# A gated feed-forward kernel on one core: TensorE in program order, and a new order of the first stage

## The chip, the cores and the metric

The kernel runs on one core of one Trainium2 chip. The metric is the device time of one execution in microseconds. Before the change it is 559.42 us, the median of three runs (558.79 to 560.9).

The engines are called PE or TensorE (matmuls; PEld is its weight load), DVE or VectorE, ACT or ScalarE, POOL or GpSimd, and SP or SyncE, which here only issues transfers.

## The reference

x is 2048 x 1024, w_gate and w_up are 1024 x 3584, w_down is 3584 x 1024, all in bf16.

```python
g = jnp.einsum("bsd,df->bsf", x, w_gate)
u = jnp.einsum("bsd,df->bsf", x, w_up)
h = _gelu(g) * u
return jnp.einsum("bsf,fd->bsd", h, w_down)
```

## The kernel before

The kernel replaces eight block products by seven (a Strassen-Winograd scheme), at the price of sums of blocks, which other engines make. It goes over x in two passes of 1024 rows, each of two chunks of 512. A **unit** makes two blocks of 128 columns of h for both chunks, for gate and up: 7 groups of 8 matmuls. `t` are sums of blocks of x (made once a pass on VectorE), `s` are sums of blocks of weights (made for each unit, on GpSimd from the second unit on). Then a **down** stage multiplies h by w_down in the same manner.

The tile framework builds the program. For engines listed in `ORDER` the instructions stay in program order; the builder orders the others itself, before the program runs. TensorE and ScalarE are not in the list:

```python
ORDER = {ENG.SP, ENG.DVE, ENG.Pool}
...
ctx.enter_context(tc.manual_schedule(engines=ORDER))
...
kpool = ctx.enter_context(tc.tile_pool(name="k", bufs=SLOTS))   # 52 slots for sums and copies
wpool = ctx.enter_context(tc.tile_pool(name="w", bufs=3))       # three units' weights
bank = [psum.tile([P, N], f32, name=f"bank{i}") for i in range(8)]
even, odd, cc, dd = bank[0:2], bank[2:4], bank[4:6], bank[6:8]
```

The sums. `dve` and `pool` are tensor_tensor on VectorE and GpSimd (recorded as L90 and L93), `cast` and `snap` are ScalarE copies (L102 and L107), all matmuls outside the transposes are L111.

```python
def make_t(xT):
    t1, t2, t3, t4, tb = [], [], [], [], []
    for k in range(KH):                       # KH = 4
        b11, b12, b22 = xT[0][:, k], xT[1][:, k], xT[1][:, KH + k]
        t1.append(new(dve, b12, b11, SUB, "t1"))
        t2.append(new(dve, b22, t1[k], SUB, "t2"))
    for k in range(KH):
        t3.append(new(dve, xT[1][:, KH + k], xT[1][:, k], SUB, "t3"))
        tb.append(cast(xT[1][:, KH + k], "tb"))
    for k in range(KH):
        t4.append(new(dve, xT[0][:, KH + k], t2[k], SUB, "t4"))
    return t1, t2, t3, t4, tb
# make_s(w, eng): s1, s2, s3, s4 (two of each, on eng) and sa (two casts), in the same way
```

One unit. `e`, `c` and `d` are pairs of PSUM banks; `add(c, p1)` makes two VectorE sums.

```python
def unit(u, banks, xT, w, s, t, after_p5, aside):
    ...
    e, c, d = banks
    for i in GU: product(e[i], w[:, i, :KH, :P], b11, True)      # plain
    p1 = [snap(e[i], "p1") for i in GU]
    for i in GU: product(c[i], w[:, i, KH:, :P], b21, True)      # plain
    g, up = add(c, p1)
    for i in GU: product(e[i], s2[i], t2, False)
    times(2 * u, 0, gelu(g), up)                                 # hT <- g * up, VectorE
    aside(0)
    u2 = [snap(e[i], "u2") for i in GU]
    c = d
    for i in GU: product(c[i], s1[i], t1, True)                  # P5
    p5 = [snap(c[i], "p5") for i in GU]
    after_p5()            # next unit's s on GpSimd, the load of the weights after it
    for i in GU: product(e[i], s3[i], t3, False)
    g, up = new(dve, e[0], p5[0], ADD, "sum", dtype=f32), banks[1][1]
    dve(up, e[1], p5[1], ADD)
    for i in GU: product(c[i], s4[i], tb, False)
    times(2 * u + 1, 1, gelu(g), up)
    aside(1)
    g, up = add(c, u2)
    for i in GU: product(e[i], sa[i], t4, False)
    times(2 * u, 1, gelu(g), up)
    aside(2)
    times(2 * u + 1, 0, gelu(e[0]), e[1])
```

`aside` makes sums of w_down blocks on VectorE (`m`, three for each of 14 blocks, in the first pass), which go through a DRAM tile `td` to the down stage. `making(u)` says which of them a unit makes: one or two.

The start. Unit 0 is done without the scheme ("plain"), so that TensorE has work while the first sums are made:

```python
xn0 = load_x(0)                  # 4 transfers of 256 KB
# wf: unit 0's weights, 8 transfers of 128 KB
xn1 = load_x(1)
w = load_w(1)                    # 2 transfers of 512 KB
for _ in range(NWARM):           # 8
    nc.tensor.matmul(bank[3], lhsT=warm[:, :P], rhs=warm, start=True, stop=True)
turn(xT, xn0, 0)                 # 32 transposes to banks 4-7, copies on VectorE and ScalarE
JI = [(j, i) for j in range(2) for i in range(2)]
ps = bank[0:4]
for k in range(0, NKB, 2):
    for p, (j, i) in zip(ps, JI):
        plain(p, i, j, 0, [k, k + 1])
s = make_s(w, dve)
turn(xT, xn1, 1)
for j in range(2):
    times(j, 0, gelu(ps[2 * j]), ps[2 * j + 1])
t = make_t(xT)
ps = bank[0:2] + bank[6:8]
for p, (j, i) in zip(ps, JI):
    plain(p, i, j, 1, range(NKB))
for j in range(2):
    times(j, 1, gelu(ps[2 * j]), ps[2 * j + 1])
...
fetch_wd(0)
ahead = load_w(2)
# then the units 1 to 13 and the down stage, and the second pass
```

Of the kernel before, what the change touches and what calls it, by code (L numbers as in the profile page):

```python
# [10 lines left out]
def kernel(  # L11
# [22 lines left out]

    nc = tc.nc
    ENG = mybir.EngineType
    ORDER = {ENG.SP, ENG.DVE, ENG.Pool}
    P = nc.NUM_PARTITIONS
    bf16 = mybir.dt.bfloat16
    f32 = mybir.dt.float32  # L40
# [10 lines left out]
    NKB = Dm // P  # L51
    KH = NKB // 2
# [31 lines left out]


    bank = [psum.tile([P, N], f32, name=f"bank{i}") for i in range(8)]
    even, odd, cc, dd = bank[0:2], bank[2:4], bank[4:6], bank[6:8]

    def dve(out, a, b, op):
        nc.vector.tensor_tensor(out=out, in0=a, in1=b, op=op)  # L90
# [4 lines left out]
    def new(eng, a, b, op, name, shape=None, dtype=None):  # L95
        t = slot(shape or [P, N], dtype or f32r, name)
        eng(t, a, b, op)
        return t

    def cast(src, name, shape=None):  # L100
        t = slot(shape or [P, N], f32r, name)
        nc.scalar.copy(out=t, in_=src)  # L102
        return t
# [10 lines left out]

    def load_w(u):
        f0 = u * 2 * P
        w = wpool.tile([P, 2, NKB, 2 * P], bf16, name="w")
        for i, src in enumerate((w_gate, w_up)):  # L120
            nc.sync.dma_start(
                out=w[:, i],
                in_=src[:, f0 : f0 + 2 * P].rearrange("(ko ki) f -> ki ko f", ki=P),
            )
        return w

    def make_t(xT):
        t1, t2, t3, t4, tb = [], [], [], [], []
        for k in range(KH):
            b11, b12, b22 = xT[0][:, k], xT[1][:, k], xT[1][:, KH + k]  # L130
            t1.append(new(dve, b12, b11, SUB, "t1"))
            t2.append(new(dve, b22, t1[k], SUB, "t2"))
        for k in range(KH):
            t3.append(new(dve, xT[1][:, KH + k], xT[1][:, k], SUB, "t3"))
            tb.append(cast(xT[1][:, KH + k], "tb"))
        for k in range(KH):
            t4.append(new(dve, xT[0][:, KH + k], t2[k], SUB, "t4"))
        return t1, t2, t3, t4, tb

    def make_s(w, eng):  # L140
        s1, s2, s3, s4, sa = [], [], [], [], []
        sh = [P, KH, P]
        for i in range(2):
            a21, a22 = w[:, i, :KH, P:], w[:, i, KH:, P:]
            s1.append(new(eng, a21, a22, ADD, "s1", sh))
        for i in range(2):
            s2.append(new(eng, s1[i], w[:, i, :KH, :P], SUB, "s2", sh))
        for i in range(2):
            s3.append(new(eng, w[:, i, :KH, :P], w[:, i, :KH, P:], SUB, "s3", sh))
            sa.append(cast(w[:, i, KH:, P:], "sa", sh))  # L150
        for i in range(2):
            s4.append(new(eng, w[:, i, KH:, :P], s2[i], SUB, "s4", sh))
        return s1, s2, s3, s4, sa

    def gelu(src):
        g = slot([P, N], f32, "g")
# [4 lines left out]
        dve(hT[:, fb // NJ, fb % NJ, c, :], g, u, MUL)  # L161

    def unit(u, banks, xT, w, s, t, after_p5, aside):
        s1, s2, s3, s4, sa = s
        t1, t2, t3, t4, tb = t
        GU = range(2)

        def product(ps, lhs, rhs, start):
            for k in range(KH):
                matmul(ps, lhs[:, k, :], rhs[k], start and k == 0, k == KH - 1)  # L170

        def add(ps, other):

            g = new(dve, ps[0], other[0], ADD, "sum", dtype=f32)
            dve(ps[1], ps[1], other[1], ADD)
            return g, ps[1]

        b11 = [xT[0][:, k, :] for k in range(KH)]
        b21 = [xT[0][:, KH + k, :] for k in range(KH)]
        e, c, d = banks  # L180
        for i in GU:
            product(e[i], w[:, i, :KH, :P], b11, True)
        p1 = [snap(e[i], "p1") for i in GU]
        for i in GU:
            product(c[i], w[:, i, KH:, :P], b21, True)
        g, up = add(c, p1)
        for i in GU:
            product(e[i], s2[i], t2, False)
        times(2 * u, 0, gelu(g), up)
        aside(0)  # L190
        u2 = [snap(e[i], "u2") for i in GU]
        c = d
        for i in GU:
            product(c[i], s1[i], t1, True)
        p5 = [snap(c[i], "p5") for i in GU]
        after_p5()
        for i in GU:
            product(e[i], s3[i], t3, False)
        g, up = new(dve, e[0], p5[0], ADD, "sum", dtype=f32), banks[1][1]
        dve(up, e[1], p5[1], ADD)  # L200
        for i in GU:
            product(c[i], s4[i], tb, False)
        times(2 * u + 1, 1, gelu(g), up)
        aside(1)
        g, up = add(c, u2)
        for i in GU:
            product(e[i], sa[i], t4, False)
        times(2 * u, 1, gelu(g), up)
        aside(2)
        times(2 * u + 1, 0, gelu(e[0]), e[1])  # L210
# [84 lines left out]
    for j in range(NJ):  # L295
        at(AT12[j], load12, j)
        at(AT12S[j], make12, j)
        at(AT73[j] - 3, fetch73, j)
        at(AT73[j], make73, j)
        at(52 + 0.7 * j, load4, j)  # L300
        at(56 + 0.5 * j, make_sa, j)
    moves = [(c, ko) for ko in range(NKB) for c in range(2)]
    sa = {}

# [111 lines left out]
            )  # L416
    xn1 = load_x(1)
    w = load_w(1)
    for _ in range(NWARM):
        nc.tensor.matmul(bank[3], lhsT=warm[:, :P], rhs=warm, start=True, stop=True)  # L420
    turn(xT, xn0, 0)

    def plain(ps, i, j, c, kos):
        for ko in kos:
            matmul(
                ps,
                wf[:, i, ko, j * P : (j + 1) * P],
                xT[c][:, ko, :],
                ko == 0,
                ko == NKB - 1,  # L430
            )

    JI = [(j, i) for j in range(2) for i in range(2)]
    ps = bank[0:4]
    for k in range(0, NKB, 2):
        for p, (j, i) in zip(ps, JI):
            plain(p, i, j, 0, [k, k + 1])
    s = make_s(w, dve)
    turn(xT, xn1, 1)
    for j in range(2):  # L440
        times(j, 0, gelu(ps[2 * j]), ps[2 * j + 1])
    t = make_t(xT)
    ps = bank[0:2] + bank[6:8]
    for p, (j, i) in zip(ps, JI):
        plain(p, i, j, 1, range(NKB))
    for j in range(2):
        times(j, 1, gelu(ps[2 * j]), ps[2 * j + 1])

    def making(u):

        return {1: [0], 2: [1, 2], 3: [3], 4: [4, 5]}.get(u, [u + 1] if 4 < u < NU - 1 else [])

    nxt = {}
    fetch_wd(0)
    ahead = load_w(2)
    for ip in range(NPASS):
        for u in range(1 if ip == 0 else 0, NU):
            js = making(u) if ip == 0 else []

            def prepare():  # L460
                nonlocal ahead
                nxt["w"], nxt["s"] = ahead, None
                if u + 1 < NU:
                    nxt["s"] = make_s(ahead, pool)
                if u + 2 < NU:
                    ahead = load_w(u + 2)
                for j in making(u + 1) if ip == 0 else []:
                    fetch_wd(j)

            def aside(part):  # L470
                if len(js) == 1:
                    keep(js[0], part)
                elif js and part != 1:
                    for n in range(3):
                        keep(js[part // 2], n)
                    if part == 0:
                        store_made(js[0])

            if ip == 0 and making(u - 1):
                store_made(making(u - 1)[-1])  # L480
            unit(u, (odd if u % 2 else even, cc, dd), xT, w, s, t, prepare, aside)
            if u + 1 < NU:
                w, s = nxt["w"], nxt["s"]

        last = ip == NPASS - 1
        got, nxt = {}, {}

        def more(step):

            nonlocal ahead  # L490
            if last:
                return
            if step == 0:
                xT[:] = new_x()
            if step >= 0 and step % 2 == 0 and step // 2 < len(moves):
                c, ko = moves[step // 2]
                r0 = (2 * (ip + 1) + c) * N
                nc.sync.dma_start_transpose(
                    out=xT[c][:, ko, :], in_=x2[r0 : r0 + N, ko * P : (ko + 1) * P]
                )  # L500
            if step == 50:
                got["w"], ahead = load_w(0), load_w(1)
            if step == 58:
                got["s"] = make_s(got["w"], dve)
            if step == 62:
                got["t"] = make_t(xT)

        down(ip, even + cc, dd + odd, last, more)
        even, odd, cc, dd = odd, even, dd, cc
        if not last:  # L510
            w, t, s = got["w"], got["t"], got["s"]
# [29 lines left out]
```

## Time and profile before

| | value |
|---|---|
| median time | 559.42 us |
| span of the profiled execution | 558.6 us |
| TensorE busy | 541.4 us (97%) |
| VectorE busy | 367.7 us (66%) |
| ScalarE busy | 247.5 us (44%) |
| GpSimd busy | 242.6 us (43%) |
| moved by transfers | 93.30 MB, mean 167 GB/s |

The page of a profile lists the busy time of each engine, then the span in 40 equal slices (a digit is the busy share in tenths), and groups of instructions by line, engine and tile. Further views give the waits of an engine by releaser ("waited for: us in total, times, longest us"), the instructions in order of time (start, duration, what it is), and the busy time in chosen stretches.

### The profile page before, as it was taken

What the parts mean: (1) busy time and instruction counts of PE and PEld (TensorE: products, weight loads), DVE (VectorE), ACT (ScalarE), POOL (GpSimd) and SP (SyncE); (2) the same over time, 40 slices, a digit from 0 to 9 for tenths busy, and PEclk for the clock granted to TensorE, in tenths of its full rate; (3) what the DMA queues carried; (4) which work ended last, traced back from release to release, by engine and by line L of the source; (5) the groups of instructions that cost most, each with busy time, mean ns of one, the idle gap of its engine ahead of it and who ended that gap; (6) DMA issues with size and microseconds to landing.
All of it is one profiled execution on the core that took longest, in us unless ns stands there. A gap on an engine that the chain in (4) does not pass through costs nothing.

```text
span 558.6 us, 7422 instructions
## 1 busy us (share of the span) xinstructions
PE 541.4 (97%) x2398; PEld 381.1 (68%) x2432; DVE 367.7 (66%) x533; ACT 247.5 (44%) x430; POOL 242.6 (43%) x206
## 2 busy tenths in 40 slices
PE   5969999999999999999999999999999999999997
PEld 3436766767667764788877777777667775478885
DVE  1797978788777778388695545555545548757730
ACT  2514545455555521044535555555555551114531
POOL 0433596998788100000048766677777700000000
PEclk9998999999999999999999999999999999999999
DMA  8533667776666299977935333222222049554562
GB/s 254 160 85 122 215 219 235 216 226 172 169 171 208 100 306 301 281 231 213 297 118 152 88 108 103 79 76 76 76 76 75 2 143 377 176 196 123 162 203 90
DMA packets 104391, 93.30 MB, mean 167 GB/s; under 512 B 12960, under 2 KB 88736, under 8 KB 104352
## 3 DMA queue, kind: packets, MB, share of 16 engines
q1 hardware_dynamic: 104352, 92.82, 55.8%
q8 instruction: 20, 0.33, 0.3%
q14 instruction: 19, 0.16, 0.1%
HBM read 75.50 MB, written 15.20 MB: 162 GB/s over the span
## 4 chain that ended last, share of the span: by engine, by line
PE 89%; DMA 4%; DVE 4%; issue 1%; ACT 1%; SPq 0%; DVEq 0%; ACTq 0%
PE bank L111 88%; DMA td<-m 2%; DVE m L90 2%; DMA xn<-in_x_dram 2%; DVE hT L90 1%; DVE t L90 1%; ACT g L157 0%; DVE sum L90 0%; PE bank L399 0%; SPq L391 0%; DVE xT L402 0%; ACT sa L102 0%; ACT st L362 0%; ACT u L107 0%; SPq L411 0%
## 5 line engine op out<-in xcount | busy, mean ns | idle before, releaser
L93 POOL TENSOR_TENSOR s<-w 128x512 fp32r<-128x512 bf16 x100 | 122.7, 1246 | 203.5 <-DVE t L90 103.0
L111 PE MATMUL bank<-t,s 128*128 128x512 f32 x648 | 162.1, 405 | 4.9 <-DVE hT L90 4.4
L111 PEld LDWEIGHTS bank<-t,s 128*128 128x128 f32 x648 | 123.1, 191 | 35.0 <-DVE hT L90 4.8
L111 PE MATMUL bank<-xT,w 128*128 128x512 bf16 x468 | 111.6, 380 | 2.1 <-DVE xT L402 0.2
L157 ACT ACTIVATE g<-sum 128x512 f32<-128x512 f32 x81 | 51.2, 632 | 108.8 <-DVE sum L90 106.5
L107 ACT COPY p<-bank 128x512 f32<-128x512 f32 x124 | 70.4, 590 | 53.4 <-PE bank L111 52.3
L90 DVE TENSOR_TENSOR hT<-g,bank 128x512 bf16<-128x512 f32 x112 | 76.7, 687 | 18.6 <-PE bank L111 8.5
L111 PEld LDWEIGHTS <-w 128*128 128x128 bf16 x496 | 44.2, 98 | 60.5 <-issue 14.5
L90 DVE TENSOR_TENSOR sum<-bank,p 128x512 f32<-128x512 f32 x54 | 37.2, 688 | 72.4 <-PE bank L111 72.3
L93 POOL TENSOR_TENSOR s<-w,s 128x512 fp32r<-128x512 bf16 x50 | 61.8, 1260 | 0.0
L93 POOL TENSOR_TENSOR s<-s,w 128x512 fp32r<-128x512 f32 x50 | 60.9, 1240 | 0.4 <-PE bank L111 0.3
L111 PE MATMUL bank<-q 128*128 128x512 f32 x240 | 59.1, 389 | 0.0
L111 PE MATMUL bank<-t,sa 128*128 128x512 f32 x216 | 58.6, 413 | 0.0
L111 PE MATMUL bank<-tb,s 128*128 128x512 f32 x216 | 53.4, 389 | 0.0
L111 PEld LDWEIGHTS bank<-q 128*128 128x128 f32 x240 | 45.1, 188 | 9.3
L111 PE MATMUL bank<-raw,hT 128*128 128x512 bf16 x218 | 48.7, 379 | 0.3
L111 PEld LDWEIGHTS bank<-t,sa 128*128 128x128 f32 x216 | 40.7, 188 | 10.5
L111 PEld LDWEIGHTS bank<-tb,s 128*128 128x128 f32 x216 | 40.7, 188 | 8.6
L107 ACT COPY u<-bank 128x512 f32<-128x512 f32 x62 | 35.3, 588 | 22.6 <-PE bank L111 22.2
L90 DVE TENSOR_TENSOR q<-hT 128x512 fp32r<-128x512 bf16 x56 | 38.4, 687 | 10.3 <-PE bank L111 9.1
L102 ACT CAST tb<-raw 128x512 fp32r<-128x512 bf16 x28 | 17.0, 625 | 61.2 <-PE bank L111 31.4
L90 DVE TENSOR_TENSOR bank<-bank,p 128x512 f32<-128x512 f32 x54 | 37.6, 696 | 8.3 <-PE bank L111 6.9
(42 smaller groups left out, 455.0 us busy)
## 6 DMA issues: line engine op xcount, KB each, us to landing
raw<-in_w_down_dram SPq DMA_DIRECT2D x84, 256.0 KB, 4.8
q<-td SPq DMA_DIRECT2D x60, 256.0 KB, 5.1
w<-in_w_gate_dram SPq DMA_DIRECT2D x27, 512.0 KB, 5.9
w<-in_w_up_dram SPq DMA_DIRECT2D x27, 512.0 KB, 7.2
td<-m SPq DMA_DIRECT2D x14, 768.0 KB, 4.5
w<-td SPq DMA_DIRECT2D x6, 1024.0 KB, 8.1
out_dram<-st SPq DMA_DIRECT2D x32, 128.0 KB, 2.5
xn<-in_x_dram SPq DMA_DIRECT2D x8, 256.0 KB, 4.7
```

Of the source, the lines that this page charges most:

```text
L90: nc.vector.tensor_tensor(out=out, in0=a, in1=b, op=op)
L93: nc.gpsimd.tensor_tensor(out=out, in0=a, in1=b, op=op)
L102: nc.scalar.copy(out=t, in_=src)
L107: nc.scalar.copy(out=t, in_=ps)
L111: nc.tensor.matmul(ps, lhsT=lhs, rhs=rhs, start=start, stop=stop, skip_group_check=True)
L157: nc.scalar.activation(g, src, ACT.Gelu_apprx_tanh)
```

## The change

It keeps every product and every sum and changes their order. TensorE joins the engines that keep program order. In the first stage the transposes of the second chunk of x are put in the middle of the first plain chunk, between its two halves. The first s and t sums are made name by name in the order in which unit 1 uses them, with the evacuations of the plain banks between them, and s4 and t4 only inside unit 1. ScalarE keeps program order in this stage. The banks are assigned so that unit 1 takes the banks of the first plain chunk. The load of unit 2's weights is moved from the start into unit 1, and is issued by ScalarE after the p1 copies; with it moves the start of GpSimd's sums, which need these weights. The w_down sums are spread anew: one a unit from unit 2 on, two in units 6, 8 and 10. Two lists of steps in the down stage are shifted.

```diff
-    ORDER = {ENG.SP, ENG.DVE, ENG.Pool}
+    ORDER = {ENG.SP, ENG.DVE, ENG.Pool, ENG.PE}
-    even, odd, cc, dd = bank[0:2], bank[2:4], bank[4:6], bank[6:8]
+    even, odd, cc, dd = bank[6:8], bank[0:2], bank[2:4], bank[4:6]
...
-    def load_w(u):
+    def load_w(u, queue=nc.sync):
...
+            if queue is not nc.sync:
+                tc.keep_in_program_order(got)
...    (make_s and make_t: the same sums, made by name: s.make("s1", "s2"); t1 all four, then t2 all four, ...)
         p1 = [snap(e[i], "p1") for i in GU]
+        aside(-1)
...
-        at(52 + 0.7 * j, load4, j)
-        at(56 + 0.5 * j, make_sa, j)
+        at(49 + 0.65 * j, load4, j)
+        at(54 + 0.55 * j, make_sa, j)
...
+    s, t = sums_s(w, dve), sums_t(xT)
+    with tc.manual_schedule(engines={ENG.Activation}):
+        for _ in range(NWARM):
+            nc.tensor.matmul(bank[3], lhsT=warm[:, :P], rhs=warm, start=True, stop=True)
+        turn(xT, xn0, 0)
+        plain(bank[0:4], 0, range(0, KH))
+        turn(xT, xn1, 1)
+        plain(bank[0:4], 0, range(KH, NKB))
+        s.make("s1", "s2")
+        t.make("t1", "t2")
+        finish(bank[0:4], 0)          # two gelu, two hT
+        t.make("t3", "tb")
+        s.make("s3", "sa")
+        plain(bank[4:8], 1, range(NKB))
+        finish(bank[4:8], 1)
...
-        return {1: [0], 2: [1, 2], 3: [3], 4: [4, 5]}.get(u, [u + 1] if 4 < u < NU - 1 else [])
+        steps = [[], []]
+        for n in range(2, NU - 1):
+            first = sum(map(len, steps))
+            steps.append([first, first + 1] if n in (6, 8, 10) else [first])
+        return steps[u] if u < NU - 1 else []
...
-    fetch_wd(0)
-    ahead = load_w(2)
+    ahead = None
...
             def aside(part):
+                nonlocal ahead
+                if ahead is None:
+                    ahead = load_w(2, nc.scalar)
+                if part == 0 and "s4" not in s:
+                    s.make("s4")
+                    t.make("t4")
+                if part < 0:
+                    return
```

More of the change, by code (lines that the diff above doesn't have):

```diff
@@ L120, in load_w @@
         for i, src in enumerate((w_gate, w_up)):
-            nc.sync.dma_start(
+            got = queue.dma_start(
                 out=w[:, i],
@@ L124, in load_w @@
             )
-        return w
-    def make_t(xT):
[L128 to L138, printed above, removed]
@@ L140, in make_s @@
-    def make_s(w, eng):
[L141 to L153, printed above, removed]
+            if queue is not nc.sync:
+                tc.keep_in_program_order(got)
@@ new lines, in load_w, with make, sums_t @@
+        return w
+    class Sums(dict):
+        def make(self, *names):
+            for name in names:
+                self[name] = self["how"][name](self)
+    def sums_t(xT):
+        K = range(KH)
+        lo, hi = [[xT[c][:, k] for k in K] for c in range(2)], [
+            [xT[c][:, KH + k] for k in K] for c in range(2)
+        ]
+        return Sums(
+            how={
+                "t1": lambda q: [new(dve, lo[1][k], lo[0][k], SUB, "t1") for k in K],
+                "t2": lambda q: [new(dve, hi[1][k], q["t1"][k], SUB, "t2") for k in K],
+                "t3": lambda q: [new(dve, hi[1][k], lo[1][k], SUB, "t3") for k in K],
+                "t4": lambda q: [new(dve, hi[0][k], q["t2"][k], SUB, "t4") for k in K],
+                "tb": lambda q: [cast(hi[1][k], "tb") for k in K],
+            }
+        )
@@ new lines, in sums_s @@
+    def sums_s(w, eng):
+        GU = range(2)
+        sh = [P, KH, P]
+        a11, a21 = [[w[:, i, :KH, h : h + P] for i in GU] for h in (0, P)]
+        a12, a22 = [[w[:, i, KH:, h : h + P] for i in GU] for h in (0, P)]
+        return Sums(
+            how={
+                "s1": lambda q: [new(eng, a21[i], a22[i], ADD, "s1", sh) for i in GU],
+                "s2": lambda q: [new(eng, q["s1"][i], a11[i], SUB, "s2", sh) for i in GU],
+                "s3": lambda q: [new(eng, a11[i], a21[i], SUB, "s3", sh) for i in GU],
+                "s4": lambda q: [new(eng, a12[i], q["s2"][i], SUB, "s4", sh) for i in GU],
+                "sa": lambda q: [cast(a22[i], "sa", sh) for i in GU],
+            }
+        )
@@ L155, in gelu @@
+    def make_t(xT):
+        t = sums_t(xT)
+        t.make("t1", "t2", "t3", "tb", "t4")
+        return t
+    def make_s(w, eng):
+        s = sums_s(w, eng)
+        s.make("s1", "s2", "s3", "sa", "s4")
+        return s
     def gelu(src):
@@ L163, in unit @@
     def unit(u, banks, xT, w, s, t, after_p5, aside):
-        s1, s2, s3, s4, sa = s
-        t1, t2, t3, t4, tb = t
         GU = range(2)
@@ L187, in unit @@
         for i in GU:
-            product(e[i], s2[i], t2, False)
+            product(e[i], s["s2"][i], t["t2"], False)
         times(2 * u, 0, gelu(g), up)
@@ L193, in unit @@
         for i in GU:
-            product(c[i], s1[i], t1, True)
+            product(c[i], s["s1"][i], t["t1"], True)
         p5 = [snap(c[i], "p5") for i in GU]
@@ L197, in unit @@
         for i in GU:
-            product(e[i], s3[i], t3, False)
+            product(e[i], s["s3"][i], t["t3"], False)
         g, up = new(dve, e[0], p5[0], ADD, "sum", dtype=f32), banks[1][1]
@@ L201, in unit @@
         for i in GU:
-            product(c[i], s4[i], tb, False)
+            product(c[i], s["s4"][i], t["tb"], False)
         times(2 * u + 1, 1, gelu(g), up)
@@ L206, in unit @@
         for i in GU:
-            product(e[i], sa[i], t4, False)
+            product(e[i], s["sa"][i], t["t4"], False)
         times(2 * u, 1, gelu(g), up)
@@ L418 @@
     w = load_w(1)
[L419 to L447, printed above, removed]
-    def making(u):
-        return {1: [0], 2: [1, 2], 3: [3], 4: [4, 5]}.get(u, [u + 1] if 4 < u < NU - 1 else [])
+    def plain(ps, c, kos):
+        for k in range(kos.start, kos.stop, 2):
+            for p, (j, i) in zip(ps, [(j, i) for j in range(2) for i in range(2)]):
+                for ko in (k, k + 1):
+                    matmul(
+                        p,
+                        wf[:, i, ko, j * P : (j + 1) * P],
+                        xT[c][:, ko, :],
+                        ko == 0,
+                        ko == NKB - 1,
+                    )
@@ new lines, in finish @@
+    def finish(ps, c):
+        for j in range(2):
+            times(j, c, gelu(ps[2 * j]), ps[2 * j + 1])
+    s, t = sums_s(w, dve), sums_t(xT)
[13 more added lines that the diff above has]
+        finish(bank[4:8], 1)
```

## The prediction

> **What bounds the kernel now.** First the page's busy totals and its forty slices.
>
> ```profile
> PE 541.4 (97%) x2398; PEld 381.1 (68%) x2432; DVE 367.7 (66%) x533; ACT 247.5 (44%) x430; POOL 242.6 (43%) x206
> ...
> PE   5969999999999999999999999999999999999997
> PEclk9998999999999999999999999999999999999999
> ```
>
> TensorE is the bound, and it is full everywhere except in the first three slices (14 us each) and the last. Busy is not yet useful, though: a busy TensorE at half clock looks the same, so I read the waits of TensorE next, and then the first 50 us in stretches (columns: PE, PEld, DVE, ACT, POOL busy, granted clock, DMA share, GB/s).
>
> ```profile
> PE bank L399 <- DMA xn<-in_x_dram: 5.1, 2, 4.8
> PE bank L111 <- DVE hT L90: 4.4, 1, 4.4
> PE bank L420 <- DVE warm L382: 1.2, 1, 1.2
> ```
>
> ```profile
> 7.20:11.96 4.76, 0.00 (x0) 0.00 (x1) 0.02 (x1) 1.01 (x1) 0.00 (x0) 1.00 0.91 282
> ...
> 36.60:41.00 4.40, 0.01 (x1) 0.01 (x1) 4.40 (x9) 0.00 (x0) 0.00 (x0) 0.82 0.00 0
> ```
>
> ```profile
> 12.00:15.40 3.40, 3.06 (x25) 2.52 (x27) 0.00 (x0) 0.33 (x1) 0.00 (x0) 0.51 1.05 305
> ...
> 41.00:46.20 5.20, 5.20 (x12) 3.95 (x13) 3.12 (x5) 4.17 (x8) 0.00 (x0) 0.50 0.59 202
> ...
> 100.00:545.00 445.00, 443.23 (x1954) 316.53 (x1980) 295.37 (x439) 202.17 (x353) 193.09 (x163) 1.00 0.56 165
> ```
>
> There are two holes. From 7.2 to 12.0 TensorE waits for the second chunk of x, because the builder put the second transposes ahead of the first plain products. From 36.6 to 41.0 it waits for VectorE, which has a queue of 24 sums (s and t) before it frees the plain banks (hT). After each hole the clock is 0.5 for 3.4 and 5.2 us. From 100 to 545 us only 1.8 of 445 us are idle: nothing to win there, only something to lose.
>
> Why is VectorE late at 41? Its timeline beside GpSimd's:
>
> ```profile
> 29.76 1.54 DVE L90 TENSOR_TENSOR t<-xT,t 128x512 fp32r<-128x512 bf16 x1
> 31.22 1.65 DVE L90 TENSOR_TENSOR t<-xT,xT 128x512 fp32r<-128x512 bf16 x1
> 32.90 0.69 DVE L90 TENSOR_TENSOR t<-xT,t 128x512 fp32r<-128x512 bf16 x1
> ...
> 39.65 1.28 DVE L90 TENSOR_TENSOR hT<-g,bank 128x512 bf16<-128x512 f32 x2
> ```
>
> ```profile
> 29.14 3.18 POOL L93 TENSOR_TENSOR s<-w,s 128x512 fp32r<-128x512 bf16 x2
> ```
>
> While GpSimd makes the second unit's sums (20.9 to 32.3) a t sum takes about 1.55 us instead of 0.69. hT, which reads PSUM, keeps its pace (1.28 for two).
>
> [...]
>
> **The change part by part.** A unit is 7 groups of 8 matmuls; in the steady stage it takes 12.62 us (VectorE's p5 sum at 160.31 and again at 172.93), so a matmul costs 12.62/56 = 0.2254 and a group 1.8 us. All estimates use these.
>
> *The yardstick.* In the kernel before, unit 1's last group runs from 50.55 to 52.75, with 12 matmuls of unit 2 already done ahead of it: 12 x 0.2254 = 2.7, so unit 1 alone is worth 52.75 - 2.7 = 50.05 us. From there to the last matmul (555.25) are 505.2 us, and the tail is 3.35. If the rest keeps its pace, the gain is 50.05 less the new end of unit 1.
>
> *First chunk and transposes.* Up to 7.2 nothing changes. The first half of plain chunk 0 (16 matmuls, 3.6 us) needs the last copy of xT0, which ends at 7.21 + 1.01 = 8.2, and four weight pieces: issued at 2.6 to 4.1, median 3.9 to landing, so there by 8.0. It runs 8.3 to 11.9, in the hole. The second chunk of x lands from 11.96; its last piece was issued at about 8.4 and took at most 5.6, so by 14.0. The 32 transposes end at 14.7 to 15.0. Second half: to 18.6. Plain chunk 1 in banks 4 to 7 (32 matmuls, 7.2 us): to 25.8. No idle stretch now exceeds 1.2 us, so I expect no half clock.
>
> *First sums.* VectorE can start when unit 1's weights have landed. Before, the second half landed at 17.5, with 0.5 MB of w_down issued between; bytes moved at about 0.32 MB/us there, so without them I take 16.1. Then, at 0.6 to 0.69 each: s1 second, two s2, four t1, four t2 (11 x 0.63 = 6.9) to 23.0; two hT to 24.3, so banks 0 to 3 are free before unit 1 wants them at 25.8. Four t3 and two s3 (3.8) to 28.1, two more hT to 29.4, before P5 wants banks 4 and 5 at 31.2. The 4.4 us hole is gone, with 1.5 to 1.8 us to spare.
>
> *Unit 1.* Undisturbed it is 25.8 + 12.6 = 38.4. But s4 and t4 now stand inside it: after the two c sums and hT (end 31.2) come two s4 (32.5) and four t4, then the sum of e with p5, which the last group must wait for; that group is due at 36.6. At 0.62 each, t4 ends at 35.0 and the sum at 35.6: no wait.
>
> *The later weights.* Their issue stands after two p1 copies on ScalarE, at about 28.2. Unit 3's weights, on SyncE, may go just ahead, since plain chunk 1 frees their buffer at 25.8. In the trace such a load (issued 31.2) had all landed after 5 to 6 us. So GpSimd starts between 32.5 and 34, right beside t4. Four t4 at 1.55 are 6.2, ending at 38.7 instead of 35.0; the sum then ends at 39.3 and the last group starts 2.8 us late: unit 1 ends at 41.2. I choose nearer to that than to 38.4: 40.7. GpSimd needs 4 x 1.4 = 5.6 us to s2, so about 39; unit 2 asks for it 5.4 us after its own start at about 40.7, so that is no wait.
>
> *Sum.* 50.05 - 40.7 = 9.35 us: 559.4 - 9.4 = 550.0. It can be counted from causes too: idle 4.8 + 4.4, half clock 1.7 + 2.6, short waits about 1, together 14.5; less new waits of 1.1 (at 7.2), about 0.9 (transposes arriving) and 2.3 (t4) leaves 10.2, a little more than the yardstick.
>
> *The rest.* Strict order in the units takes out the four plain matmuls that the builder had put between the s4 and the t4 groups, so the sums of e with p5 have 0.9 us less. In the timeline VectorE had been idle 0.90 before such a sum (160.31) and starts it 0.2 after its matmul; sum and in-place sum take 1.3 together and the s4 group covers 1.8, so it fits, except perhaps where six w_down sums lie in one unit (now units 6, 8, 10 instead of 2 and 4). load4 and make_sa come about 2 steps earlier in a stage that is 100% busy: nothing.
>
> **The rivals.** First: *strict order stalls the units*. If each of 27 units lost 0.3 us, that is 8 us, and the time stays at 558. For it: VectorE is 76% and GpSimd 74% busy from 100 to 200. Against: the 0.90 us of slack just named, and the down stage was already almost in program order without waits. Second: *the wait is moved, not removed*: weights of unit 1 land no earlier than 17.5 and t4 meets GpSimd in full. Then everything on VectorE is 1.4 later, unit 1 ends at about 44, and the time is 553. Third: *the transfer is hidden*: GpSimd starts after t4, unit 1 ends at 38.4, and the time is 547.8. Fourth: half clock stays[...]: 1.7 us more, 551.7.
>
> **Range and chances.** Predicted 550.0; 547.0 (third rival and a little from the short waits) to 554.0 (second rival plus small stalls). 2% faster is below about 548.3, which needs unit 1 to end before 39: 0.22. Slower by over 2% needs a stall in every unit that I find no cause for: 0.02. Within 2%: 0.76.
>
> **What would show it.** Right: no TensorE wait over 2 us before the tail; plain products at 8.3; clock 1.0 from 12 to 46; unit 1's last group ending near 41, with VectorE t sums near 1.5 us just before it and a TensorE wait on VectorE of 1 to 3 us; 445 us of middle stage with at most 2 us idle. Wrong: a clock of 0.5 early, a wait on hT near 26 or 31, or many short TensorE waits on VectorE or ScalarE from 50 us on.

## The result, and the profile after

The changed kernel takes 551.61 us (median of 4 runs, 550.05 to 554.33) against 559.62 for the kernel before (here the median of 4 runs), 8.0 us less; the ratio is 0.986, with a 95% interval of 0.981 to 0.991. The span of the profiled execution fell from 558.6 to 549.9, by 8.7 us.

The page of the changed kernel: the busy times are nearly the same, but the first slices are fuller and the clock row shows no 8.

```profile
PE 536.8 (98%) x2397; PEld 381.6 (69%) x2432; DVE 360.5 (66%) x533; ACT 247.6 (45%) x430; POOL 242.2 (44%) x206
...
PE   7999999999999999999999999999999999999997
...
PEclk9999999999999999999999999999999999999999
```

The waits of TensorE in the changed kernel (in total, times, longest):

```profile
PE bank L111 <- DVE sum L90: 3.4, 5, 1.3
...
PE bank L111 <- ACT xT L424: 1.1, 1, 1.1
PE bank L111 <- DMA raw<-in_w_down_dram: 0.8, 1, 0.8
...
```

The waits of 4.8 and 4.4 us are gone; 0.7 is left for x. New are 1.1 (the plain products wait for the last copy of xT0), five waits for sums of VectorE, and 0.8 for a block of w_down. The stretches (columns as in the prediction) show the start full and at full clock, and a small loss from 100 to 200, where the kernel before was idle for 0.5 us:

```profile
7.20:12.00 4.80, 3.65 (x22) 1.84 (x21) 0.65 (x1) 1.35 (x2) 0.00 (x0) 1.00 0.90 282
12.00:15.40 3.40, 2.48 (x35) 1.85 (x34) 1.26 (x2) 1.01 (x1) 0.00 (x0) 1.00 1.10 316
...
41.00:46.20 5.20, 5.15 (x24) 3.50 (x24) 4.09 (x6) 2.94 (x6) 5.20 (x6) 1.00 0.37 106
...
100.00:200.00 100.00, 97.36 (x426) 67.48 (x433) 79.53 (x112) 47.59 (x85) 61.73 (x48) 1.00 0.74 227
```

The place where the prediction expected the one larger new wait, in the timeline of the changed kernel: four t4 sums, GpSimd's first sums of unit 2 beside them, and the t4 group of TensorE.

```profile
33.80 3.46 DVE L90 TENSOR_TENSOR t<-xT,t 128x512 fp32r<-128x512 bf16 x4
...
34.92 1.19 POOL L93 TENSOR_TENSOR s<-w 128x512 fp32r<-128x512 bf16 x1 [33.62 <-DMA w<-in_w_gate_dram]
...
37.92 2.11 PE L111 MATMUL bank<-t,sa 128*128 128x512 f32 x8 [1.30 <-DVE sum L90]
```

Four t4 take 3.46 us, where four t sums alone take 2.49 (the row at 22.18 of the same timeline, and f1 below); TensorE waits 1.30. Unit 1 ends at 37.92 + 2.11 = 40.03.

The account, with the same yardstick for both kernels:

| stretch | before | after | gain |
|---|---|---|---|
| start to the end of unit 1 | 50.05 | 40.03 | 10.0 |
| from there to the last stage | 491.6 | 493.6 | -2.0 |
| last stage (56 matmuls) | 13.60 | 12.86 | 0.7 |
| tail | 3.35 | 3.37 | 0.0 |

### The profile page after: what moved, and what is told of

Same layout as the page of the kernel before. It is cut to its first block, busy times and chain, and to the rows that moved or that the text cites. A ratio compares the mean times of both kernels' runs of the same rounds, so it can differ in the third digit from the quotient of the medians.

```text
span 549.9 us, 7422 instructions
## 1 busy us (share of the span) xinstructions
PE 536.8 (98%) x2397; PEld 381.6 (69%) x2432; DVE 360.5 (66%) x533; ACT 247.6 (45%) x430; POOL 242.2 (44%) x206
## 4 chain that ended last, share of the span: by engine, by line
PE 60%; DMA 1%; issue 0%; ACT 0%
PE bank L111 60%; DMA raw<-in_w_down_dram 1%; ACT st L382 0%
## 5 line engine op out<-in xcount | busy, mean ns | idle before, releaser
L93 POOL TENSOR_TENSOR s<-w 128x512 fp32r<-128x512 bf16 x100 | 124.6, 1264 | 196.4 <-DVE t L90 99.7
L111 PE MATMUL bank<-t,s 128*128 128x512 f32 x648 | 157.1, 398 | 0.0
L111 PEld LDWEIGHTS bank<-t,s 128*128 128x128 f32 x648 | 121.8, 188 | 27.7
L111 PE MATMUL bank<-xT,w 128*128 128x512 bf16 x467 | 106.4, 379 | 3.0 <-ACT xT L424 1.1
L111 PEld LDWEIGHTS <-w 128*128 128x128 bf16 x496 | 46.4, 98 | 59.9 <-issue 7.2
L93 POOL TENSOR_TENSOR s<-s,w 128x512 fp32r<-128x512 f32 x50 | 58.1, 1182 | 0.0
L111 PE MATMUL bank<-t,sa 128*128 128x512 f32 x216 | 54.0, 392 | 3.4 <-DVE sum L90 3.4
```

The costliest lines, as they stand in the source:

```text
L93: nc.gpsimd.tensor_tensor(out=out, in0=a, in1=b, op=op)
L111: nc.tensor.matmul(ps, lhsT=lhs, rhs=rhs, start=start, stop=stop, skip_group_check=True)
```

## The experiments

The theory, A: the gain is made in the first 46 us. Two holes of TensorE and the half clock after them go, because the second transposes stand where x arrives, the evacuations stand between the first sums, and GpSimd starts after the t sums; program order is the means. Rival B: a fixed order of TensorE is itself the gain. The new banks and ScalarE's program order in the first stage were not tried singly. A second question is what the middle lost: three w_down sums in a row (D), or VectorE's load as such (E). Each ratio is to runs of the kernel before on the same chip; their medians were 559.6 to 560.1.

| kernel | median us | ratio to before, 95% interval | end of unit 1, profiled |
|---|---|---|---|
| changed kernel | 551.61 | 0.986 (0.981 to 0.991) | 40.0 |
| e1 program order alone | 561.59 | 1.002 (1.000 to 1.004) | 50.1 |
| e2 weights early | 557.36 | 0.995 (0.993 to 0.997) | 46.9 |
| e3 builder orders TensorE | 558.28 | 0.997 (0.996 to 0.999) | 47.0 |
| e4 transposes first | 553.30 | 0.988 (0.985 to 0.991) | 41.8 |
| e5 old order of sums | 552.39 | 0.987 (0.984 to 0.989) | 41.9 |
| e6a w_down sums 2, 1, 3 | 563.26 | 1.007 (1.005 to 1.009) | 42.2 |
| e6b two buffers m | 552.80 | 0.988 (0.985 to 0.990) | 44.7 |
| e7 weights later | 550.47 | 0.984 (0.982 to 0.986) | 39.6 |
| f1 later, two buffers | 547.11 | 0.977 (0.976 to 0.979) | 37.5 |
| f2 latest, two buffers | 547.60 | 0.979 (0.977 to 0.980) | 38.1 |
| f3 old lists | 554.23 | 0.989 (0.987 to 0.992) | 39.3 |
| f4 changed kernel again | 551.62 | 0.985 (0.983 to 0.987) | 40.4 |

(The end of unit 1 in e3 is less 12 matmuls of unit 2 that run ahead of it, as for the kernel before.)

**e1, program order alone.** The kernel before with

```diff
-    ORDER = {ENG.SP, ENG.DVE, ENG.Pool}
+    ORDER = {ENG.SP, ENG.DVE, ENG.Pool, ENG.PE}
```

> The kernel before with TensorE in program order and nothing else. Theory A (the gain is made in the first 46 us, by transposes in the middle, by the order of the sums and by GpSimd starting late, and program order alone is only the means): the first hole is filled by plain chunk 0, but the second transposes then come after it and their copies on VectorE stand behind eight s sums that wait for weights until 17.5; a new hole of about 6 us opens near 18 to 25, the t sums still meet GpSimd, unit 1 ends near 48 against 50.05, span 556 to 558 (before 558.6). Rival B (a fixed order of TensorE is itself what gains): span 550 to 552, like the changed kernel.

561.59 us, no gain. Its waits of TensorE:

```profile
PE bank L111 <- DVE xT L402: 6.3, 1, 6.3
PE bank L111 <- DVE hT L90: 1.6, 1, 1.6
PE bank L111 <- DMA q<-td: 1.6, 2, 1.4
```

The first hole is filled, and the next one opens: the copies of the second chunk stand on VectorE behind eight s sums. The clock is 0.5 from 23 to 28. Unit 1 ends at 50.1, as before, and the span grows by 3.5 us behind it. Of these only 0.4 lie between unit 1 and the last stage, though TensorE waits there 0.5 us twice for sums and 0.9 for w_down; 3.1 lie in the last stage, which takes 16.7 us instead of 13.60: it waits 1.6 us for td, and its last 43 matmuls take 11.62 us, 270 ns each, where 225 is the pace. B falls. A was too hopeful by 2 us at unit 1 and did not foresee the 3.5.

**e2, unit 2's weights early.** The changed kernel with

```diff
     w = load_w(1)
+    ahead = load_w(2)
...
-    ahead = None
```

> The changed kernel with unit 2's weights loaded right after unit 1's, as before the change. Theory A: GpSimd runs from about 20 to 33 beside t1 to t3, each of those sums takes about 1.5 us instead of 0.62, hT of the first plain chunk ends at about 30 instead of 25.9, TensorE waits 4 to 6 us in all, with half clock perhaps 8; span 555 to 558 against 549.9. Rival C (VectorE has slack enough, the late load matters little): span within 1 us of 549.9, and the 1.30 us wait before the t4 group is gone.

557.36 us, 5.7 more than the changed kernel. The timeline:

```profile
19.55 6.33 DVE L90 TENSOR_TENSOR t<-xT,xT 128x512 fp32r<-128x512 bf16 x4
...
25.81 6.32 DVE L90 TENSOR_TENSOR t<-xT,t 128x512 fp32r<-128x512 bf16 x4
...
32.05 1.27 DVE L90 TENSOR_TENSOR hT<-g,bank 128x512 bf16<-128x512 f32 x2
...
32.78 4.00 PE L111 MATMUL bank<-xT,w 128*128 128x512 bf16 x9 [6.74 <-DVE hT L90]
```

GpSimd makes its sums from 19.31 to 31.57. Four t sums take 6.3 us beside them instead of 2.49, twice over: 7.7 us, and hT is late by about that (32.05 against 24.59). TensorE waits 6.74 and then runs nine matmuls in 4.00 us (the clock is 0.56 from 32.7 to 38). Theory A holds, rival C falls: this part alone is worth 5.7 us.

**e3, the builder orders TensorE.** The changed kernel without ENG.PE in ORDER.

> The changed kernel without TensorE in program order; in the built program the builder moves three of four blocks of second transposes ahead of the first plain products. Theory A: the hole from 7.5 to 12 us is back with half clock after it, plain products start at about 15; unit 1 ends 3 to 5 us later than 40.0 (the wait for t4 goes), the small waits of units 8 to 11 may go (2 us): span 551.5 to 554. Rival B': the builder's order is as good, span within 1 us of 549.9.

558.28 us; the span is 556.4, where A expected 551.5 to 554, and rival B' falls too. The hole at the transposes is back, and there is another:

```profile
11.86 1.03 PE L419 MATMUL bank<-ident,xn 128*128 128x128 bf16 x8 [4.35 <-DMA xn<-in_x_dram]
...
39.56 1.03 PE L111 MATMUL bank<-xT,w 128*128 128x512 bf16 x4 [2.16 <-DMA w<-in_w_gate_dram]
41.14 3.16 PE L111 MATMUL bank<-xT,w 128*128 128x512 bf16 x7 [0.56 <-DMA w<-in_w_up_dram]
```

The builder puts the plain products of unit 2 ahead of the last groups of unit 1. That was harmless while the weights came early. With late weights they wait 2.7 us and hold everything behind them, and a lower clock follows (seven matmuls in 3.16 us; it is 0.68 from 41 to 46). So program order is a condition for loading late, although alone it gains nothing.

**e4, transposes first.**

```diff
         turn(xT, xn0, 0)
-        plain(bank[0:4], 0, range(0, KH))
         turn(xT, xn1, 1)
+        plain(bank[0:4], 0, range(0, KH))
         plain(bank[0:4], 0, range(KH, NKB))
```

> The changed kernel with the second transposes ahead of the whole first plain chunk, TensorE still in program order. Theory A: TensorE idle from 7.5 to 12.5 or so, then transposes to 15.3, clock 0.5 until about 15.5, plain products from 15.3: 3.6 us of work moved behind, 0.5 to 1.5 us of half clock; the 1.3 us wait for t4 goes. Unit 1 ends at 43 to 44, span 552.5 to 554. Rival: VectorE sets the end of unit 1 anyway (it is busy without a gap from 18 to 40), so the hole costs nothing: span within 0.7 of 549.9.

553.30 us. TensorE waits 3.40 and 0.55 us for x, as expected, but unit 1 ends only 1.8 us later, not 3 to 4. Its span, 550.7, is below what A gave.

```profile
38.22 1.18 POOL L93 TENSOR_TENSOR s<-w 128x512 fp32r<-128x512 bf16 x1 [36.91 <-DMA w<-in_w_gate_dram]
```

TensorE reaches the s2 group of unit 1 3.4 us later (32.31 against 28.96), but about half of that comes back: the p1 copies are later too, and with them the issue of unit 2's weights, so GpSimd starts at 38.22, after the t4 sums (2.49 us), and the wait of 1.30 before the t4 group is gone. The rival falls: from 15.27 to the end of unit 1 TensorE waits for no sum. So 1.7 us is what filling the first hole pays as long as it also brings GpSimd beside t4.

**e5, the old order of the sums.** All s, then hT of the first plain chunk, all t, then hT of the second:

```diff
-        s.make("s1", "s2")
-        t.make("t1", "t2")
+        s.make("s1", "s2", "s3", "sa", "s4")
         finish(bank[0:4], 0)
-        t.make("t3", "tb")
-        s.make("s3", "sa")
+        t.make("t1", "t2", "t3", "tb", "t4")
```

> The changed kernel with the sums of unit 1 made in the old order: eight s, then hT of the first plain chunk, sixteen t, then hT of the second. GpSimd stays late. Theory A (evacuations between the sums matter by themselves): hT of the second plain chunk ends at about 35 instead of 30.7, P5 waits 3 to 4 us for banks 4 and 5, the wait for t4 goes; unit 1 ends near 42, span 551.5 to 553. Rival: VectorE's total work sets the end of unit 1, so its order does not matter: span within 0.7 of 549.9.

552.39 us, span 552.0, as A expected; the rival gave at most 550.6. In its timeline:

```profile
32.44 1.20 PE L111 MATMUL bank<-t,s 128*128 128x512 f32 x4 [1.69 <-DVE hT L90]
34.78 3.44 PE L111 MATMUL bank<-t,s 128*128 128x512 f32 x8 [1.14 <-ACT u L107]
```

The wait for hT is 1.7 instead of 3 to 4, but a second one, for ScalarE's copies, and a stretch at a lower clock (eight matmuls in 3.44; the clock is 0.75 from 32.5 to 36 and 0.79 from there to 40) follow it. Unit 1 ends 1.8 us later. The times of the two kernels overlap too much (550.05 to 554.33 and 551.96 to 553.76) to show this; the traces do.

**e6a, six w_down sums split 2, 1, 3.** Same buffers, in units 6, 8 and 10:

```diff
-                elif js and part != 1:
-                    for n in range(3):
-                        keep(js[part // 2], n)
-                    if part == 0:
+                elif js:
+                    for j, n in (((0, 0), (0, 1)), ((0, 2),), ((1, 0), (1, 1), (1, 2)))[part]:
+                        keep(js[j], n)
+                    if part == 1:
                         store_made(js[0])
```

> The changed kernel with the six w_down sums of units 6, 8, 10 split two, one, three over the three places instead of three, none, three. Theory D (three sums in a row beside GpSimd, 4.7 us, make VectorE late for the sum with p5): the TensorE waits in units 8 and 10 (0.42 and 0.64) go, those in units 9 and 11 (0.63 and 0.42), which follow a 3.3 us wait of VectorE for the one buffer m, stay. Span about 1 us less, 548.5 to 549.5. Rival E (total load of VectorE in those units): all four waits stay within 0.3.

563.26 us: much slower, against both theories. The four old waits are gone, but in the unit after each of the three (7, 9 and 11) there is a worse one (2.81, 3.74 and 2.80 us). The first of them:

```profile
107.54 1.65 DVE L90 TENSOR_TENSOR m<-raw 128x512 fp32r<-128x512 bf16 x1 [1.28 <-DMA td<-m]
...
113.63 0.63 ACT L178 ACTIVATE g<-sum 128x512 f32<-128x512 f32 x1 [6.32 <-DVE sum L90]
...
114.88 2.06 PE L111 MATMUL bank<-t,s 128*128 128x512 f32 x8 [2.81 <-ACT u L107]
```

The first three sums end later, so the store of the one buffer m is later, and the second three wait for it and run beside GpSimd (4.8 us). Then the chain passes over three engines: VectorE's sum is late, ScalarE's gelu waits 6.32 for it, the u2 copies stand behind the gelu, and TensorE waits for u2. So the trace points to the place of the store, which neither theory had; it was not tried singly.

**e6b, two buffers m.** Two sums in each of the three places, two buffers, and 49 slots to make room:

```diff
-    SLOTS = 52
+    SLOTS = 49
-    mpool = ... bufs=1
+    mpool = ... bufs=2
-                elif js and part != 1:
-                    for n in range(3):
-                        keep(js[part // 2], n)
-                    if part == 0:
-                        store_made(js[0])
+                elif js:
+                    for n in (2 * part, 2 * part + 1):
+                        keep(js[n // 3], n % 3)
+                        if n == 2:
+                            store_made(js[0])
```

> The changed kernel with the w_down sums two at a time in all three places and two buffers m, paid for with 49 instead of 52 slots. Theory D: all four TensorE waits in units 8 to 11 (2.1 us in all) go, and VectorE's waits for the store of m too; span 547.5 to 548.5. Rival E: the waits stay; rival F: three slots fewer make GpSimd or transfers late and new waits appear.

552.80 us. From 100 to 200 us TensorE is idle for 0.00: E falls, and the waits are gone as D said. The edit changes the split and the number of buffers together; which of the two it takes was not taken apart. But the start became worse:

```profile
31.99 1.44 POOL L93 TENSOR_TENSOR s<-w 128x512 fp32r<-128x512 bf16 x1 [30.69 <-DMA w<-in_w_gate_dram]
...
33.91 6.32 DVE L90 TENSOR_TENSOR t<-xT,t 128x512 fp32r<-128x512 bf16 x4
...
40.89 3.35 PE L111 MATMUL bank<-t,sa 128*128 128x512 f32 x7 [5.34 <-DVE sum L90]
```

GpSimd starts 3 us earlier than in the changed kernel, all four t4 meet it, take 6.32 us, and TensorE waits 5.34, with a clock of 0.50 after it (40.9 to 45). Two things came together: unit 2's weights were issued at 25.93 instead of 27.63 in this execution, and with fewer slots a w_down transfer was issued later (29.84 instead of 26.98). The load took 6.1 us instead of 7.3. How much is due to each was not taken apart. Rival F was right that the start suffers, but it is GpSimd early, not late.

**e7, unit 2's weights later.** The load moves from the p1 copies to behind the t4 sums in the program:

```diff
-                if ahead is None:
-                    ahead = load_w(2, nc.scalar)
                 if part == 0 and "s4" not in s:
                     s.make("s4")
                     t.make("t4")
+                    ahead = load_w(2, nc.scalar)
```

> The changed kernel with unit 2's weights issued only after the t4 sums are queued, some 4 us later than 27.6. Theory A: GpSimd starts at about 38, the four t4 take 2.5 us instead of 3.46, the TensorE wait of 1.30 before the t4 group falls to about 0.3; span about 1 us less. Rival G: GpSimd's sums or ScalarE's casts of unit 2 come late in turn, and a wait of 1 us or more opens in unit 2; span the same or more.

550.47 us (550.23 to 550.82). The load is issued at 30.85 instead of 27.63, but GpSimd starts at 34.93, as in the changed kernel: it takes 4.1 us to there instead of 7.3. In the changed kernel unit 3's weights and w_down are issued from 25.89 to 28.7, around it, and the transfers move 318 GB/s from 27.6 to 34.8. Here they are issued from 25.29 to 27.8, and at that rate, an estimate, their 1.5 MB are through by about 30.2. In the kernel before, such a load with nothing else under way (31.18) landed its first half after 3.8 us. t4 still takes 3.46, and the wait is 0.92. So A's size was wrong here; no wait appears in unit 2, so G falls.

**f1, later weights and two buffers m**, the edits of e7 and e6b together.

> The changed kernel with both edits that helped in part: unit 2's weights issued after the t4 sums are queued, and the w_down sums two at a time with two buffers m and 49 slots. If the waits of units 8 to 11 come from three w_down sums in a row and the wait for m, they are gone (2 us less than 550.5), and if the 5.3 us wait of the two-buffer kernel came only from GpSimd starting 3 us earlier beside t4, it is gone as well: TensorE waits 1.5 us or less before the first t4 group; median 547.5 to 549. If instead the three missing slots caused it, the wait of several us is still there; median 551 to 553.

547.11 us (546.79 to 547.81): better than both kernels, 4.5 less than the changed one.

```profile
32.27 2.49 DVE L90 TENSOR_TENSOR t<-xT,t 128x512 fp32r<-128x512 bf16 x4
...
34.54 0.62 ACT L102 CAST sa<-w 128x512 fp32r<-128x512 bf16 x1 [1.57 <-DMA w<-in_w_gate_dram]
...
34.69 1.16 POOL L93 TENSOR_TENSOR s<-w 128x512 fp32r<-128x512 bf16 x1 [33.38 <-PE bank L111]
...
35.41 2.11 PE L111 MATMUL bank<-t,sa 128*128 128x512 f32 x8
```

GpSimd starts as the last t4 ends, four t4 take 2.49, and the t4 group does not wait: the wait of e6b is gone with the same 49 slots. The view puts GpSimd's start down to a matmul, but ScalarE's cast of the same weights starts only 0.15 us earlier, when they land: the transfer all but sets it still. Against e7, GpSimd is not later (34.69, there 34.93); t4 is earlier (32.27, there 33.33), and so is VectorE already at the hT before (27.86, there 28.94). That fits unit 1's weights landing 1.07 us earlier in this execution: in e7 and in the changed kernel t4 starts 15.83 and 15.84 us after the second s1, which waits for them (17.50 and 17.96), and this puts it at 16.43 here, an estimate. Whether the edits have a part in that is not shown. From 100 to 200 us TensorE is idle for 0.00. Of the 3.9 us between the profiled spans of e7 and f1 (548.8 and 544.9), 2.0 lie before the end of unit 1 and 1.8 between it and the last stage, where the waits are gone.

**f2, still later.** The load stands behind the u2 copies instead.

> As the kernel with later weights and two buffers, but the weights of unit 2 issued after the u2 copies, some 2 us later still. If only GpSimd beside t4 counts, t4 takes 2.5 us and the TensorE wait before the t4 group is under 0.4: 0.5 to 1 us less than that kernel. If the other side of the trade bites (ScalarE's casts of unit 2 wait for these weights in front of the gelu, or GpSimd's s2 is late), a wait of 0.5 to 2 us opens in unit 2 and it is equal or slower.

547.60 us (546.84 to 548.42), no better: t4 takes 2.49 as well, the profiled execution waits 0.52, and unit 2 takes 13.0 us instead of 12.6. It does not decide between its two cases.

**f3, the old lists of the down stage.**

```diff
-        at(49 + 0.65 * j, load4, j)
-        at(54 + 0.55 * j, make_sa, j)
+        at(52 + 0.7 * j, load4, j)
+        at(56 + 0.5 * j, make_sa, j)
```

> The changed kernel with the old steps for load4 and make_sa. In the last stage the kernel before took 13.60 us for 56 matmuls, the changed one 12.86, and the kernel with program order alone waited 1.6 us there for the td pieces. If that is the lists' doing, about 1.5 us of waits for td come back near 534 and the time is 0.7 to 1.8 us more than the changed kernel; if the load is hidden anyway, the last stage takes 12.9 us and the time is the same.

554.23 us, 2.6 more. In the last stage:

```profile
533.02 3.04 PE L111 MATMUL bank<-q,sa 128*128 128x512 f32 x12
537.74 0.47 PE L111 MATMUL bank<-q,sa 128*128 128x512 f32 x1 [1.67 <-DMA q<-td]
538.42 10.01 PE L111 MATMUL bank<-q,sa 128*128 128x512 f32 x43 [0.22 <-DMA q<-td]
```

The stage takes 15.4 us instead of 12.86, which is 2.5 of the 2.6. The builder's order in the kernel before lived with the same lists (13.60); program order waits for these pieces, here as in e1, and the earlier load takes the wait away.

**f4, the changed kernel again.**

> The changed kernel once more, for its scatter beside the two kernels with later weights. If the changed kernel's spread (550.05 to 554.33) comes from a race between unit 2's weights and t4, it spreads over 3 to 4 us again, and this profile may show another wait before the first t4 group than 1.30 us; the kernels with later weights spread over 1 us or less. If the spread is of the chip, all four spread alike.

551.62 us (549.91 to 552.68).

```profile
33.22 4.45 DVE L90 TENSOR_TENSOR t<-xT,t 128x512 fp32r<-128x512 bf16 x4
...
34.17 1.36 POOL L93 TENSOR_TENSOR s<-w 128x512 fp32r<-128x512 bf16 x1 [32.87 <-DMA w<-in_w_gate_dram]
...
38.33 2.11 PE L111 MATMUL bank<-t,sa 128*128 128x512 f32 x8 [2.44 <-DVE sum L90]
```

The same program waits 2.44 here and 1.30 in the first profile: GpSimd starts 0.95 us after the first t4 here and 1.12 there, and four t4 take 4.45 and 3.46. The other profiles fall in line: 6.32 where GpSimd starts 1.9 us before t4 (e6b), 3.46 where it starts 1.4 and 1.6 after it (f3, e7), 2.49 at 2.4 and 2.7 (f1, f2). So the wait is a race between two landings: in the changed kernel, e6a and e7 the first t4 starts 15.8 us after the second s1, which waits for unit 1's weights (16.8 in e6b), and GpSimd starts with unit 2's. The two kernels in which t4 is free of GpSimd, and e7, spread over 0.6 to 1.6 us, this program over 2.8 and 4.3. That the scatter comes from this race is not shown: the runs are few, and e7, where t4 still meets GpSimd, spreads least.

## Why the prediction was right, and where it was not

It said 550.0, in 547.0 to 554.0; measured 551.61. The mechanism of the start was right; the step that failed is *The rest*.

- *The yardstick and the two holes*: right. Unit 1 ends at 40.03 (predicted 40.7); plain products start at 8.67 (8.3), the transposes end at 15.5 (14.7 to 15.0), unit 1 follows plain chunk 1 at about 26 without a wait, and the clock is 1.00 all through.
- *First sums*: the estimate that unit 1's weights land at 16.1 without the w_down transfers failed: the second s1 starts at 17.96 (17.55 before). This profile is the latest one: in five others with the same loads (e4 to e7) it starts between 16.66 (e5) and 17.59 (e6a), and in f1 at about 16.43, in all of them later than estimated. Why they do not land earlier stays open. It cost nothing at hT (24.59 to 25.9, and TensorE does not wait for it), but it used up the spare time and made t4 late. This was the second rival's first half.
- *The later weights*: right in mechanism, with GpSimd at 34.92 where 32.5 to 34 was said. The term "2.8 us late" measured 1.30 and 2.44 in two executions, and 5.34 where GpSimd started at 32. It depends on when a transfer lands, so no single number was to be had.
- *The rest*: this step failed in both its parts. "It fits, except perhaps where six w_down sums lie in one unit": it does not fit there, and also not in the unit after, where VectorE waits 3.3 us for the store of m. The four waits are 0.42, 0.63, 0.64 and 0.42, 2.1 us together, and e6b and f1 show that two buffers, with two sums in each place, remove them all. "load4 and make_sa: nothing": f3 shows 2.6 us in the changed kernel. That I read "100% busy" as nothing to win was the error; the old last stage took 13.60 us for 56 matmuls, which is 243 ns for one, the new one 230, where 225 is the pace. The row reads as busy for 13.39 of the 13.60 us; what held the matmuls in it is not shown.
- *Rivals*: the first did not come. The middle lost 2.0 us and not 8, and most of it is not strict order: with strict order and the old spread of the w_down sums it loses 0.4 (e1), with the builder's order and the new spread 1.6 (e3). The fourth (half clock early) did not come.
- *Two readings* were off without harm. The hT shown at 39.65 does not run beside GpSimd, whose sums had ended at 32.3; the hT at 23.93 does, and takes 1.27 for two. And unit 2 asks for s2 after two groups, 3.6 us, not 5.4; in the trace s2 is made by 40.5, soon enough.

The start gave 10.0 instead of 9.35, the rest took 1.3 instead of nothing; the total came out near because both were small against the 9 us, and partly by luck: the gain of 0.7 in the last stage was not expected either.

## What to carry to other kernels

Fixing TensorE's order gained nothing by itself here (e1: 561.59 against 559.87) and can bring waits that a builder's order did not have (td in e1 and f3); it pays when loads and sums are placed so that each arrives just before its turn, and the late load here needs it (e3). Where VectorE's sums are on the path, start GpSimd's after them: here four took 2.49 us alone and 6.3 beside them. A start that hangs on the landing of a transfer moves (unit 1's weights by 1.3 us between the profiles of the changed kernel and e5); tying it to the last sum would be the next thing to try, and no run here did. After such a change look for waits of half a microsecond in the middle and for a stage whose time per matmul is above the pace (243 ns against 225 in the last stage before), even though the engine reads as busy.

## What the runs showed of the hardware

- Four t sums, with both inputs in SBUF, took 2.49 us alone and 6.3 beside GpSimd sums, 2.5 times as long (e2, e6b), while hT, which reads a PSUM bank, kept 0.69 for one (e6b at 41.55, with GpSimd busy from 41.21 to 43.5).
- Half clock did not follow from the length of a wait alone. The stretch of e6a after its wait of 2.32 us (the clock is the third value from the end):

```profile
38.50:42.00 3.50, 3.48 (x9) 2.50 (x10) 3.15 (x5) 1.74 (x3) 3.50 (x4) 0.52 0.11 27
```

and the stretch of f4 after its wait of 2.44 us:

```profile
38.30:42.00 3.70, 3.67 (x16) 2.23 (x17) 3.44 (x6) 2.23 (x4) 3.70 (x5) 1.00 0.10 23
```

Nine matmuls in one, sixteen in the other. Within e6a, too, waits of 2.81 and 2.80 us are followed by eight matmuls in 2.06 and in 3.05 us. After the waits of 4.35 to 6.74 us (before, e1, e2, e3, e6b) the clock was 0.50 to 0.56 each time. What decides after the shorter ones is not shown.
- A 1 MB load issued 3.2 us later landed at the same time (e7: GpSimd starts on it at 34.93, in the changed kernel at 34.92), with the other loads issued 3 us and more before it, where they had been issued from 1.7 us before to 1 us after it.
